# Retention recurrence in 64-token steps, with k in diagonal blocks and crossbar transposes from the fifth chunk on

**The chip, the cores and the metric.** One core of one Trainium2 chip. The metric is device microseconds of one execution; for each kernel the median of its runs is given, with the runs of the kernel before on the same chip beside it. Spans and times inside a trace are some 1.7 us shorter than the run's time.

## The reference

```python
# batch 8, heads 8, sequence 576, head_dim 64; d_model 512, d_ff 1536; float32
scores = q @ k.T / sqrt(64)
D[i, j] = gamma[h] ** (i - j) if i >= j else 0       # gamma[h] = 1 - 2 ** (-5 - h)
ret = (scores * D) @ v                               # per head
x = ret.transpose(0, 2, 1, 3).reshape(4608, 512)
out = (1 / (1 + exp(-(x @ w_gate))) * (x @ w_val)) @ w_out
```

Both kernels run the attention as a recurrence over chunks of 128 tokens, five to a batch (the last is a half chunk of 64). `gamma ** i` is multiplied into q and `gamma ** -j` into k, so that what is left of D is a triangle. Per chunk: scores (k against q), output (state times q, plus v times masked scores), and the state (sum of k times v). Chunks 0 to 3 are done in another way, which the change leaves alone. The rest of TensorE's time is the feed-forward part, in blocks of 128 to 512 tokens, between whose matmuls the chunk phases are placed. All matmuls are bf16.

## The kernel before

Heads are handled in pairs (two heads of 64 fill 128 rows or columns). Chunks 4 to 9 work in half-array tiles, on q and k that TensorE transposed. From chunk 10 on (`EARLY`), q and k are cast to bf16 on GpSimd, transposed by the DMA crossbar, and VectorE lays k^T out in diagonal blocks of two heads (`kbd`), so that a matmul uses the whole array.

```python
def cross(s):                                    # crossbar, from chunk 10 on
    for nm, bufs in (("k", 4), ("q", 5)):
        t = att_pool.tile([P, M, P], BF16, ...)
        nc.sync.dma_start_transpose(out=t[:, :, 0:n], in_=natural[nm, s][0:n]...)

def phase_kb(s):                                 # VectorE: k^T into diagonal blocks
    for hh in range(2):
        nc.vector.tensor_copy(out=kb[p0:p0 + 64, 0:nj, :, p0:p0 + 64]..., in_=kT[p0:p0 + 64, 0:M, 0:n]...)

# phase_qk, a full chunk:
    nc.tensor.matmul(qkp[:, mm, 0:128],   lhsT=kb[:, 0, m, :], rhs=qT[:, m, 0:128], ...)
    nc.tensor.matmul(qkp[:, mm, 128:192], lhsT=kb[:, 1, m, :], rhs=qT[:, m, 64:128], ...)
# phase_pv, for each pair m:
    (state[s - 1][:, m, :], qT[:, m, 0:128]), (vb[:, 0, m, :], pt[:, m, 0:128]), (vb[:, 1, m, :], pt[:, m, 128:192])
# phase_st: one step for 128 tokens
    nc.tensor.matmul(stp[:, m, :], lhsT=ks[:, 2*m:2*m+2, :], rhs=vn[:, 2*m:2*m+2, :], ...)

order += [("t", s + 1), ("pv", s), ("qk", s + 1), ("st", s + 1)]     # from chunk 10 on, s running
LEAD_LOAD = 5       # loads run five chunks ahead, casts two
# ... (cuts)
```

All loads, stores and crossbar transposes are issued by SyncE into one queue, in program order (half of the very last store aside).

## Time and profile before

| | before |
|---|---|
| time, median (lowest to highest) | 349.19 us (347.98 to 350.13), 4 runs |
| span of the profiled run | 346.6 us |
| TensorE busy | 338.1 us |
| GpSimd busy | 160.0 us |
| VectorE busy | 180.1 us |
| DMA packets; share of the 16 engines that the one queue takes | 147,506; 75.9% |

To read it: TensorE sets the time nearly everywhere, so what counts is each stretch in which it waits. The lines are in the prediction. Times in microseconds from the span's start place every event below.

### The profile page before, as it was taken

Reading aid. Unit: us, or ns where it says so; the run is one execution under the profiler, and the core shown is the slowest. Engines: PE = TensorE matmul, PEld = TensorE weight load, DVE = VectorE, ACT = ScalarE, POOL = GpSimd, SP = SyncE. Lnnn points to the kernel's source line nnn. Section 1 sums busy time; section 2 is a strip of 40 time slices with the busy share of each in tenths; the row PEclk is TensorE's granted clock in tenths of the full one; section 3 lists DMA queues with packets and bytes.
Section 4 is the critical chain, followed back from the end, with each engine's and each line's share of the span. In section 5 each row is a group of like instructions: output and inputs, shape, how many; then the busy total and the mean of one; then the engine's idle time right before and its main releaser. Section 6 shows DMA issues by size and latency. Waiting matters only on the chain.

```text
span 346.6 us, 7262 instructions
## 1 busy us (share of the span) xinstructions
PE 338.1 (98%) x2744; PEld 195.3 (56%) x2744; DVE 180.1 (52%) x365; ACT 129.2 (37%) x250; POOL 160.0 (46%) x264
## 2 busy tenths in 40 slices
PE   8899999899999999999999999999999999999996
PEld 3565447676856556656656655554555555544443
DVE  4655555595757646616736836552764355503320
ACT  6765414344334234233234334332333243324321
POOL 7743764778538736543366855533666400000000
PEclk9999999999999999999999999999999999999999
DMA  7999999999999999929829999929794410020002
GB/s 222 315 365 269 282 262 203 243 232 163 161 199 192 176 201 209 132 95 198 150 97 191 179 194 191 179 21 212 164 173 32 121 47 0 2 91 30 2 30 91
DMA packets 147506, 54.73 MB, mean 158 GB/s; under 512 B 130960, under 2 KB 139408, under 8 KB 147472
## 3 DMA queue, kind: packets, MB, share of 16 engines
q1 hardware_dynamic: 147328, 54.15, 75.9%
q8 instruction: 21, 0.34, 0.5%
q10 hardware_dynamic: 144, 0.13, 0.1%
q14 instruction: 13, 0.11, 0.1%
HBM read 37.75 MB, written 9.44 MB: 136 GB/s over the span
## 4 chain that ended last, share of the span: by engine, by line
PE 76%; DVE 2%; ACT 0%; issue 0%; ACTq 0%
PE h L567 44%; PE op L630 22%; PE pv L471 4%; PE qk L429 2%; PE st L492 2%; DVE kbd L397 1%; PE qk L431 1%; PE op L620 1%; DVE pte L418 0%; DVE qs L249 0%; DVE sbd L338 0%; DVE gv L585 0%; PE qk L438 0%; ACT g L580 0%; DVE sb L504 0%
## 5 line engine op out<-in xcount | busy, mean ns | idle before, releaser
L567 PE MATMUL h<-xT,wg_sb 128*128 128x512 bf16 (+3 forms) x592 | 118.0, 322 | 0.1
L567 PE MATMUL h<-xT,wv_sb 128*128 128x512 bf16 (+3 forms) x592 | 118.0, 322 | 0.1
L594 DVE TENSOR_TENSOR gv<-g,h 128x512 bf16<-128x512 bf16 (+1 forms) x104 | 65.0, 625 | 69.9 <-PE h L567 67.8
L590 ACT ACTIVATE g<-h 128x512 bf16<-128x512 f32 (+1 forms) x104 | 57.0, 548 | 100.1 <-PE h L567 80.3
L630 PE MATMUL op<-wo_sb,gv 128*128 128x512 bf16 x372 | 85.6, 379 | 0.0
L567 PEld LDWEIGHTS <-wg_sb 128*128 128x128 bf16 x592 | 52.9, 98 | 38.5 <-issue 0.7
L567 PEld LDWEIGHTS <-wv_sb 128*128 128x128 bf16 x592 | 52.3, 98 | 33.0 <-DVE wv_sb L209 0.7
L239 POOL TENSOR_TENSOR ks<-k,ktab 128x512 bf16<-128x512 f32 (+1 forms) x36 | 37.4, 1040 | 59.6 <-issue 18.6
L267 POOL CAST vbd<-v 64x256 bf16<-64x256 f32 x108 | 42.9, 397 | 41.5 <-PE pv L471 36.3
L630 PEld LDWEIGHTS <-gv 128*128 128x128 bf16 x372 | 34.9, 98 | 37.6
L602 ACT COPY ob<-op 128x512 f32<-128x512 f32 x35 | 20.3, 586 | 60.5 <-PE op L630 50.5
L433 DVE TENSOR_TENSOR pt<-qk,tri 128x384 bf16<-128x384 f32 x48 | 24.5, 551 | 35.3 <-PE qk L431 35.3
L249 POOL TENSOR_TENSOR qs<-q,qtab 128x512 bf16<-128x512 f32 (+1 forms) x30 | 32.3, 1075 | 1.1 <-DMA qT<-qs 1.0
L397 DVE COPY kbd<-kT 64x512 bf16<-64x512 bf16 (+1 forms) x60 | 28.2, 470 | 0.9
L472 ACT CAST xT<-pv 128x512 bf16<-128x512 f32 (+1 forms) x36 | 19.4, 538 | 21.9 <-PE pv L471 18.8
L258 POOL CAST vn<-v 128x512 bf16<-128x512 f32 (+1 forms) x36 | 23.9, 665 | 0.0
L504 DVE TENSOR_TENSOR sb<-st,bdm 128x512 bf16<-128x512 f32 x24 | 16.5, 687 | 5.8 <-PE st L492 5.8
L580 ACT ACTIVATE g<-h 128x256 bf16<-128x256 f32 x32 | 12.3, 384 | 17.3 <-PE h L567 13.4
L471 PE MATMUL pv<-pt,vbd 128*128 128x128 bf16 (+1 forms) x216 | 17.3, 204 | 0.0
L471 PEld LDWEIGHTS <-vbd 128*128 128x128 bf16 x216 | 14.7, 98 | 3.4
L471 PE MATMUL pv<-qT,sb 128*128 128x128 bf16 (+1 forms) x96 | 13.8, 213 | 0.0
L582 DVE TENSOR_TENSOR gv<-g,h 128x256 bf16<-128x256 bf16 x20 | 8.4, 418 | 10.2 <-ACT g L580 9.9
(92 smaller groups left out, 238.7 us busy)
## 6 DMA issues: line engine op xcount, KB each, us to landing
out_dram<-ob SPq DMA_DIRECT2D x35, 256.0 KB, 2.2
v<-in_v_dram SPq DMA_DIRECT2D x28, 256.0 KB, 4.1
k<-in_k_dram SPq DMA_DIRECT2D x28, 256.0 KB, 4.5
q<-in_q_dram SPq DMA_DIRECT2D x28, 256.0 KB, 5.1
wg<-in_moe_w_gate_dram SPq DMA_DIRECT2D x12, 256.0 KB, 5.5
wv<-in_moe_w_val_dram SPq DMA_DIRECT2D x12, 256.0 KB, 5.5
wo<-in_moe_w_out_dram SPq DMA_DIRECT2D x12, 256.0 KB, 5.6
k32p<-in_k_dram SPq DMA_DIRECT2D x4, 256.0 KB, 4.7
```

The source lines that it names most:

```text
L239: nc.gpsimd.tensor_tensor(out=ks[0:n], in0=k32[0:n], in1=ktab[0:n, c, :].unsqueeze(2).to_broadcast([n, H, D]), op=ALU.mult)
L249: eng.tensor_tensor(out=qs[0:n], in0=q32[0:n], in1=qtab[0:n, c, :].unsqueeze(2).to_broadcast([n, H, D]), op=ALU.mult)
L258: nc.gpsimd.tensor_copy(out=vn[0:n], in_=v32[0:n])
L267: nc.gpsimd.tensor_copy(out=vb[hh * 64:hh * 64 + 64, j, :, hh * 64:hh * 64 + 64], in_=v32[j * 64:j * 64 + 64, hh::2, :])
L397: nc.vector.tensor_copy(out=kb[p0:p0 + 64, 0:nj, :, p0:p0 + 64].rearrange("p j m t -> p m j t"), in_=kT[p0:p0 + 64, 0:M, 0:n].rearrange("p ...
L433: nc.vector.tensor_tensor(out=pt[:, 2 * g:2 * g + 2, :], in0=qkp[:, :, 0:192], in1=tri.unsqueeze(1).to_broadcast([P, 2, 192]), op=ALU.mult)
L471: nc.tensor.matmul(pvp[:, m, a:e], lhsT=w, rhs=x, start=(i == 0), stop=(i == len(mm) - 1))
L567: nc.tensor.matmul(out, lhsT=w_sb[:, kc, fc * P:(fc + 1) * P], rhs=xT[:, kc, t0 + a:t0 + e], start=(kc == 0), stop=(kc == NKC - 1))
L590: nc.scalar.activation(out=g[:, 0:n], in_=h1[:, 0:n], func=AF.Sigmoid)
L594: nc.vector.tensor_tensor(out=gvs[some[0]][:, a:e], in0=g[:, 0:n], in1=h2[:, 0:n], op=ALU.mult)
L602: nc.scalar.copy(out=ob, in_=opp)
L630: nc.tensor.matmul(opp, lhsT=gvs[fc][:, nb * P:(nb + 1) * P], rhs=wo_sb[:, fc, :], start=(fc == 0), stop=(fc == NFC - 1))
```

## The change

Its intent: spend fewer TensorE columns on the recurrence. With steps of 64 tokens every recurrence matmul is a full-array one of 64 columns; k is cast straight into diagonal blocks, which serve both the state step and, through the crossbar, the scores, so VectorE's copies go; and chunks 4 to 9 leave the half-array form.

```diff
 def cast_k(s):
-    nc.gpsimd.tensor_tensor(out=ks[0:n], in0=k32[0:n], in1=ktab..., op=ALU.mult)
+    for j in range(n // 64):
+        for hh in range(2):
+            nc.gpsimd.tensor_tensor(out=kn[half(hh), j, :, half(hh)], in0=k32[half(j), hh::2, :], in1=ktab..., op=ALU.mult)
 def cast_v(s):          # v also twice: in diagonal blocks (vbd) and plain (vs), 8 copies of 64x256
+                if c < NC - 1:
+                    nc.gpsimd.tensor_copy(out=vs[half(hh), j], in_=v32[half(j), hh::2, :])
 def cross(s):           # k: 128x1024 through the crossbar (512 before)
+    nc.sync.dma_start_transpose(out=t[:, 0:nj]..., in_=natural["k", s][:, 0:nj]...)
-def phase_tk, phase_tq, phase_kb
 def phase_qk(s):
+    for j in range(nj):
+        for m in range(M):
+            nc.tensor.matmul(qkp[:, m, half(j)], lhsT=kT[:, j, m, :], rhs=qT[:, m, half(j)], ...)
+def phase_st(s, j):     # two steps a chunk; VectorE copies the state after each
-order.append(("qk", s + 1)); order.append(("st", s + 1))
+order.append(("qk", s + 1)); order += [("st0", s + 1), ("st1", s + 1)]
 ...
+        if kind == "qk":
+            loads_to(s + LEAD_LOAD)     # LEAD_LOAD = 5, LEAD_CAST = 2
+            casts_to(s + LEAD_CAST)     # k, q, crossbar, v
 ...
+    loads_to(7)
+    casts_to(6)
+    loads_to(8)
```

(The triangle masks, the order of the wo loads and the first placements of phases also change.)

## The prediction

> **What bounds the kernel now.** I read the page first: busy shares, slices, chain.
>
> ```profile
> PE 338.1 (98%) x2744; PEld 195.3 (56%) x2744; DVE 180.1 (52%) x365; ACT 129.2 (37%) x250; POOL 160.0 (46%) x264
> ...
> PEclk9999999999999999999999999999999999999999
> DMA  7999999999999999929829999929794410020002
> ...
> PE 76%; DVE 2%; ACT 0%; issue 0%; ACTq 0%
> ```
>
> TensorE is busy 98% of 346.6 us at full clock and carries 76% of the chain: a column less on TensorE is time off the end. But the DMA row stands at 9 up to the sixteenth slice, some 139 us. The windows by stage (columns: us, then each engine's busy time, clock, DMA share, GB/s) say where that hurts.
>
> ```profile
> 36.00:60.00 24.00, 24.00 (x222) 12.98 (x220) 13.30 (x28) 7.99 (x16) 15.65 (x23) 1.00 1.07 251
> 60.00:92.00 32.00, 29.53 (x403) 23.30 (x397) 21.98 (x57) 12.28 (x29) 23.52 (x37) 1.00 1.05 206
> 92.00:140.00 48.00, 47.86 (x380) 29.58 (x378) 29.43 (x56) 17.19 (x35) 27.27 (x44) 1.00 1.13 192
> 140.00:260.00 120.00, 120.00 (x878) 67.84 (x876) 65.20 (x122) 41.69 (x77) 64.93 (x106) 1.00 0.84 155
> 260.00:346.00 86.00, 83.34 (x501) 41.74 (x498) 30.38 (x53) 26.54 (x46) 9.26 (x16) 1.00 0.17 45
> ```
>
> From 36 to 140 us TensorE and the DMA engines are both full. After that DMA has room. The only stage with real TensorE idleness is 60 to 92 us, 2.5 us of it.
>
> The price of a matmul is read from starts, not from the mean ns of a row, which includes the pipeline. The timeline of TensorE:
>
> ```profile
> 112.88 0.28 PE L438 MATMUL qk<-qT,kbd 128*128 128x64 bf16 x4
> 112.99 0.81 PE L567 MATMUL h<-xT,wv_sb 128*128 128x384 bf16 x4
> ```
>
> Four 64-column matmuls, each with new weights, take 112.99-112.88 = 0.11 us: 28.5 ns each. By the same reading a 128-column one takes 56 ns (the first three matmuls of a pv head pair, 128+128+64 columns, repeat every 0.14 us).
>
> **What the Trainium skill says.** "TensorE: Matmul & The Clock Gate", section "Wait — 56ns, not 53.3ns?": start to start is N/2.4 + about 2.5 ns, never under about 25 ns. That gives 55.8 and 29.2 ns; the trace agrees. The same page, "Back-to-back issue gap", says a stream of weight-load and matmul pairs sustains about 81 ns at N=128; the trace does not agree (56 ns), so I use 28.5 even for runs of small matmuls. "DMA: Bandwidth & Descriptors", "Queues, rings and completion order": each DMA engine consumes one issuer's descriptors in ring order. So a transpose waits behind loads issued before it; the trace agrees, with 4.1 us from issue to landing for kT. "TensorEngine Tiling (Array Packing)", "Key Properties": changing the tiling mode drains TensorE; the change removes such switches from chunk 4 on, and I count no more for them than the measured starts contain.
>
> **The change, part by part.** TensorE, per full chunk with an incoming state, chunks 10 on: before, scores 4x128+4x64, state 4x128, output 8x128+4x64 columns: 16x56+8x28.5 = 1.12 us. After: 8 score, 8 state, 16 output matmuls, all 64 wide: 32x28.5 = 0.91. Saved 0.21; a first chunk of a batch saves 0.10 (0.90 to 28x28.5 = 0.80), a half chunk nothing. Six batches x (3x0.212+0.102) = 4.4 us. The six chunks 4 to 9 now cost 8.4 us by starts (both transposes 2.7, scores 1.8, state 1.0, output 2.9). After: three chunks at 32, one at 28, two at 12 matmuls, 148x28.5 = 4.2. Saved 4.2. The TensorE gaps there (1.48 and 0.39 us before scores that wait for qT, 0.25 before a transpose, 1.0 at 85.7 before scores that wait for kbd, 0.3 at 111.8) are 3.4 us and their causes go. TensorE's gross gain: 12.0 us, 3.4%.
>
> VectorE loses the 60 kbd copies (28.2 us) and pays two 64x256 state copies per 64 tokens (4x0.42 = 1.7 us a chunk, against 0.69): even or lighter, and 48% idle. GpSimd: k becomes four pieces, about half of the 1.04 us each (estimate from the equal rows at 64 and 128 partitions), v eight copies at 0.44 (four took 1.75), q 1.04: 2.1+3.5+1.04 = 6.6 us a full chunk, before 4.4. Some 3 us a half chunk. All 36 chunks: 28x6.6+8x3 = 209, with weights and constants about 235 us. TensorE spends about 39 us on a batch of five chunks, GpSimd 29.5: it holds in the steady part.
>
> DMA: kT doubles, from 512 to 1024 packets of 256 bytes, and chunks 4 to 9, which now use no crossbar, get it. Before a full pair is 1024 packets, after 1536. A 256 KB load of 1024 packets takes 1.2 us in the full stretches (3,200 to 3,460 packets in 4 us), so the new pair costs 1.8 us, and 0.4 for the thin stretch that the packets show around transposes: 2.2 us, a half pair 1.1. A 2 KB-packet tile (wo, a store) takes 0.7. Steady cycle: 3x1.2+2.2+0.7 = 6.5 us under TensorE's 8.5: hidden. In the full stretch it is not hidden. The timelines of GpSimd, SyncE and TensorE there, in that order:
>
> ```profile
> 35.60 1.03 POOL L239 TENSOR_TENSOR ks<-k,ktab 64x512 bf16<-64x512 f32 x1 [5.24 <-DMA k<-in_k_dram]
> ```
>
> ```profile
> 77.21 1.67 SPq L276 DMA_TRANSPOSE kT<-ks  x1
> 78.99 2.85 SPq L276 DMA_TRANSPOSE qT<-qs  x1
> ```
>
> ```profile
> 58.01 0.40 PE L412 MATMUL qk<-qT,kT 64*128 64x128 bf16 x8
> ...
> 68.36 0.40 PE L412 MATMUL qk<-qT,kT 64*128 64x128 bf16 x8 [1.32 <-ACT qT L387]
> ...
> 73.51 0.40 PE L412 MATMUL qk<-qT,kT 64*128 64x128 bf16 x8 [0.23 <-ACT qT L387]
> ```
>
> k of chunk 4 lands at 35.6; the first crossbar transpose is issued at 77.2. My prices for what lies between (rest of load 4 0.6, load 5 3.6, twelve wo 8.3, loads 6 to 13 27, six stores 4.1) sum to 43.6, so 79.2, when its packets indeed begin (79.8). Now the new order from 35.6: q4 and load 5 to 39.8; five wo 43.3; T4 (the transposes of chunk 4) 44.4; five wo 47.8; T5 50.0; two wo, loads 6, 7 58.6; T6 60.8; loads 8, 9, 10 and three stores 71.9; T7 74.1; load 11, a store, T8 80.6; load 12, T9, a store 86.0; load 13, T10 91.8; a store, load 14, T11 96.5. One us more to land. The scores of chunks 6, 7, 8 then start at 61.8, 75.1, 81.6, where they were at 58.0, 68.4, 73.5. Scores 9 follow TensorE's own work, 6.8 us later, 88.4; scores 10 wait to 92.8 (86.8 before) and scores 11 start at 97.5 (92.1 before). So at chunk 11 the new kernel is 5.4 us behind, with its early savings already spent inside the waits. From there it gains the 4.4 of the later batches and the 0.3 gap. Net +0.7: 349.6 to 350.3, call it 350.
>
> **The rivals.** First, DMA is hidden after all: loads run up to five chunks ahead, so later loads may give way and the transposes land in time. Against it: loads 8 to 11 stand in the same queue before T7 and T8. For it: the new order of wo loads shows care for this stretch. Then the 12.0 us come in: 338. Second, the supply is worse: transposes cost the 0.8 us of thinned packets that several pairs show in the trace now, and the output matmuls of the first 512 tokens wait for wo, whose casts now follow eight v copies in GpSimd's order (v5 ends about 45.6, wo 2 wanted at 43.8). Each pair 0.5 more is 3 to 4 us by chunk 11, and idle TensorE may lose its clock: 355 to 359. Third, the two state steps of a chunk: the second may not overwrite the bank until VectorE has copied the first. In a 384-token block the phases lie 1.7 us apart and the copies need 0.84, so little; if it fails, up to 0.3 us x 28 chunks = 8 us, 358. Fourth, 64-column matmuls in runs of 16 fall to weight-load pace, say 50 ns: 964x21 = 20 us. The four in a row at 28.5 speak against it.
>
> **Range and chances.** The gain is solid arithmetic, the loss an estimate of queue times with a few us either way: 350, range 341 to 359. Faster by over 2% (below 342.6) needs nearly all of the supply loss to vanish: 0.17. Slower by over 2% (above 356.6) needs the second or third rival: 0.25. Within 2%: 0.58.
>
> **What would show it.** Right: TensorE's summed time for chunks 4 on falls from 36 to 27.5 us at 28.5 ns a matmul; TensorE waits at the scores of chunks 6, 7, 8 for the transposes, several us each; between 36 and 100 us its busy share drops to about 80 to 85%, after 110 us it stays over 99%; GpSimd about 235 us busy. Wrong: no waits at those scores (first rival), waits of state matmuls on VectorE in the steady blocks (third), starts over 35 ns (fourth), or a clock below full.

## The result, and the profile after

The changed kernel takes 358.22 us (357.85 to 359.3, 4 runs) against 349.19 us: slower, ratio 1.0266, 95% interval 1.0224 to 1.0307. A ratio here is the mean time of one kernel's runs over that of the other's of the same rounds, so it is not quite the ratio of the medians.

The page of the changed kernel (span 356.7 us): busy times, the clock and DMA in 40 slices, the chain by engine.

```profile
PE 333.6 (94%) x2833; PEld 192.2 (54%) x2868; DVE 162.1 (45%) x343; ACT 126.8 (36%) x245; POOL 225.9 (63%) x447
...
PEclk9999989969989999999999999999999999999999
DMA  7999999999999999983985999999699550011002
...
PE 72%; POOL 14%; DMA 7%; issue 3%; DVE 2%; ACT 1%; SPq 1%; POOLq 0%; ACTq 0%; DVEq 0%
```

TensorE has less to do and the span is 10 us longer, so TensorE waits. GpSimd and DMA are now on the chain, and the clock falls in the sixth, ninth and twelfth slices. The windows (the first number pair is the stretch, then its length, then each engine's busy time) say when:

```profile
60.00:100.00 40.00, 29.18 (x377) 24.37 (x380) 16.31 (x48) 9.75 (x24) 37.09 (x75) 0.88 1.09 202
100.00:140.00 40.00, 39.75 (x367) 25.10 (x369) 19.91 (x43) 14.82 (x31) 31.65 (x63) 0.99 1.10 189
140.00:260.00 120.00, 118.89 (x984) 67.18 (x995) 60.74 (x119) 42.17 (x80) 91.02 (x182) 1.00 0.94 175
```

From 60 to 100 us TensorE is busy 29.2 of 40 us (GpSimd 37.1), after that nearly always. TensorE's timeline shows the same stretch as waits ahead of scores (the bracket: idle just before, and what ended it):

```profile
61.61 0.39 PE L365 MATMUL qk<-qT,kT 128*128 128x64 bf16 x8 [2.17 <-DMA qT<-qs]
...
74.84 0.58 PE L365 MATMUL qk<-qT,kT 128*128 128x64 bf16 x8 [3.71 <-DMA qT<-qs]
...
82.74 0.39 PE L365 MATMUL qk<-qT,kT 128*128 128x64 bf16 x8 [1.47 <-DMA qT<-qs]
```

These are chunks 6, 7 and 8, waiting for a crossbar transpose. Starts of the scores, from the timelines:

| scores of chunk | 6 | 7 | 8 | 9 | 10 | 11 | end of span |
|---|---|---|---|---|---|---|---|
| before | 58.0 | 68.4 | 73.5 | 81.5 | 86.8 | 92.1 | 346.6 |
| predicted after | 61.8 | 75.1 | 81.6 | 88.4 | 92.8 | 97.5 | |
| after | 61.6 | 74.8 | 82.7 | 90.8 | 96.5 | 104.2 | 356.7 |
| after, loads four ahead (last experiment) | 62.7 | 72.0 | 78.2 | 85.8 | 91.3 | 99.2 | 351.4 |

So at chunk 11 the changed kernel is 12.1 us late; by the end 10.1. The question is what makes the transposes late. Two suppliers stand before them. GpSimd casts (two of its costliest groups on the page):

```profile
L227 POOL TENSOR_TENSOR kbd<-k,ktab 64x256 bf16<-64x256 f32 x128 | 78.3, 612 | 47.4 <-PE st L398 32.7
...
L252 POOL CAST vs<-v 64x256 bf16<-64x256 f32 x112 | 44.7, 399 | 0.0
```

and the queue of SyncE, whose timeline from chunk 6's transposes to chunk 7's is

```profile
56.87 1.24 SPq L261 DMA_TRANSPOSE kT<-kbd  x1
58.20 2.12 SPq L265 DMA_TRANSPOSE qT<-qs  x1
60.41 0.53 SPq L82 DMA_DIRECT2D v<-in_v_dram  x1
...
66.84 1.48 SPq L82 DMA_DIRECT2D q<-in_q_dram  x1
68.43 3.74 SPq L261 DMA_TRANSPOSE kT<-kbd  x1
```

Between 60.41 and 68.32 stand nine load instructions, the v, k and q of chunks 8, 9 and 10. Chunk 7's q had been cast by 64.9, as GpSimd's timeline shows (the first line is chunk 7's q, the second chunk 8's):

```profile
63.82 1.04 POOL L237 TENSOR_TENSOR qs<-q,qtab 128x512 bf16<-128x512 f32 x1
70.71 1.04 POOL L237 TENSOR_TENSOR qs<-q,qtab 128x512 bf16<-128x512 f32 x1
```

Put side by side for each chunk (GpSimd's q cast ends, SyncE's k transpose is issued; k itself is cast 1.1 us before q):

| chunk | 7 | 8 | 9 | 10 | 11 |
|---|---|---|---|---|---|
| cast done | 64.9 | 71.7 | 77.3 | 81.9 | 88.8 |
| transpose issued | 68.4 | 77.8 | 84.9 | 91.7 | 97.8 |

### The profile page after: what moved, and what is told of

Same layout as the page of the kernel before. It is cut to its first block, busy times and chain, and to the rows that moved or that the text cites. A ratio compares the mean times of both kernels' runs of the same rounds, so it can differ in the third digit from the quotient of the medians.

```text
span 356.7 us, 7632 instructions
## 1 busy us (share of the span) xinstructions
PE 333.6 (94%) x2833; PEld 192.2 (54%) x2868; DVE 162.1 (45%) x343; ACT 126.8 (36%) x245; POOL 225.9 (63%) x447
## 2 busy tenths in 40 slices
DMA packets 169396, 60.27 MB, mean 169 GB/s; under 512 B 152848, under 2 KB 161296, under 8 KB 169360
## 4 chain that ended last, share of the span: by engine, by line
PE 72%; POOL 14%; DMA 7%; issue 3%; DVE 2%; ACT 1%; SPq 1%; POOLq 0%; ACTq 0%; DVEq 0%
PE h L457 41%; PE op L520 21%; POOL kbd L227 6%; POOL vbd L250 3%; POOL vs L252 2%; POOL qs L237 2%; DMA qT<-qs 2%; DMA q<-in_q_dram 2%; PE qk L365 2%; PE st L398 2%; PE pv L386 2%; PE pv L384 2%; DMA k<-in_k_dram 1%; DMA q32p<-in_q_dram 1%; DVE sbd L404 1%
## 5 line engine op out<-in xcount | busy, mean ns | idle before, releaser
L227 POOL TENSOR_TENSOR kbd<-k,ktab 64x256 bf16<-64x256 f32 x128 | 78.3, 612 | 47.4 <-PE st L398 32.7
L520 PE MATMUL op<-wo_sb,gv 128*128 128x512 bf16 x356 | 84.1, 379 | 0.8
L367 DVE TENSOR_TENSOR pt<-qk,tri 128x512 bf16<-128x512 f32 (+1 forms) x36 | 22.7, 630 | 72.0 <-PE qk L365 71.7
L404 DVE CAST sbd<-st 64x256 bf16<-64x256 f32 x112 | 47.0, 420 | 14.9 <-PE st L398 12.5
L250 POOL CAST vbd<-v 64x256 bf16<-64x256 f32 x128 | 50.7, 396 | 4.4
L252 POOL CAST vs<-v 64x256 bf16<-64x256 f32 x112 | 44.7, 399 | 0.0
L365 PE MATMUL qk<-qT,kT 128*128 128x64 bf16 x256 | 13.6, 195 | 10.4 <-DMA qT<-qs 10.4
L365 PEld LDWEIGHTS <-kT 128*128 128x128 bf16 x256 | 12.7, 99 | 17.1 <-DMA kT<-kbd 9.2
L398 PEld LDWEIGHTS <-kbd 128*128 128x128 bf16 x224 | 13.5, 100 | 13.2 <-DVE sbd L404 5.1
L386 PE MATMUL pv<-pt,vbd 128*128 128x64 bf16 x256 | 19.5, 194 | 0.0
L384 PE MATMUL pv<-qT,sbd 128*128 128x64 bf16 x228 | 18.5, 195 | 0.1
```

Source lines behind the costliest of these rows:

```text
L227: nc.gpsimd.tensor_tensor(out=kn[half(hh), j, :, half(hh)], in0=k32[half(j), hh::2, :], in1=ktab[half(j), c, hh::2].unsqueeze(2).to_broadc ...
L250: nc.gpsimd.tensor_copy(out=vb[half(hh), j, :, half(hh)], in_=v32[half(j), hh::2, :])
L252: nc.gpsimd.tensor_copy(out=vs[half(hh), j], in_=v32[half(j), hh::2, :])
L365: nc.tensor.matmul(qkp[:, m, half(j)], lhsT=kT[:, j, m, :], rhs=qT[:, m, half(j)], start=True, stop=True)
L384: nc.tensor.matmul(pvp[:, m, half(j)], lhsT=before[:, m, :], rhs=qT[:, m, half(j)], start=True, stop=False)
L386: nc.tensor.matmul(pvp[:, m, half(j)], lhsT=vb[:, j, m, :], rhs=pt[:, m, half(j)], start=before is None, stop=True)
```

## The experiments

The theory at first: the early chunks (36 to 105 us) are short of supply, GpSimd and the DMA queue together, and the rest of the change works as meant. Rivals: the lost clock is a cost of its own; the two state steps of a chunk wait for VectorE; the 64-column matmuls are slow.

### One: GpSimd without the second copies of v

Wrong result: `vs` is a constant, which takes four of eight v copies per chunk off GpSimd.

```diff
-        vs = nat_pool.tile([P, 2, M, D], BF16, tag="vs", ...)
+        vs = vs0                                  # memset once
-                if c < NC - 1:
-                    nc.gpsimd.tensor_copy(out=vs[half(hh), j], ...)
```

> The changed kernel without the four extra copies of v for the state (their tile is a constant, so the result is wrong on purpose); GpSimd then needs 5.3 us a full chunk instead of 6.9. If GpSimd's casts set when the transposes start, each of the waits at the scores of chunks 6, 7, 8 and 10 shrinks by 1.5 us or more and the whole comes to 350 us or less. If the queue of transfers sets it (transposes behind loads and other transposes), only the 2 us wait of the first output matmuls for wo goes, and the time stays at 354 to 357 us.

Measured: 357.81 us, ratio 1.0255 (1.0223 to 1.0287), which is 0.4 us less than the changed kernel and within the spread of both, although GpSimd fell from 225.9 to 188.6 us. (It lies 0.8 us above the range foreseen for the queue.) TensorE's wait for wo shrinks from 1.84 to 0.38 us, so that the scores of chunk 4 start at 46.5 us instead of 49.0, but by chunk 6 nothing is left of it (61.5 against 61.6). Chunk 7's transpose was issued at the same time as before:

```profile
68.30 4.03 SPq L261 DMA_TRANSPOSE kT<-kbd  x1
```

What follows: GpSimd by itself is not the bound.

### Two: half of k through the crossbar

Wrong result: the first 64 tokens' transposed k serves both halves.

```diff
-        nc.sync.dma_start_transpose(out=t[:, 0:nj]..., in_=natural["k", s][:, 0:nj]...)
+        nc.sync.dma_start_transpose(out=t[:, 0:1]..., in_=natural["k", s][:, 0:1]...)
-    lhsT=kT[:, j, m, :]
+    lhsT=kT[:, 0, m, :]
```

> The changed kernel with only the first 64-token half of each k tile sent through the crossbar, and used for both halves (wrong on purpose): the transposes are as small as in the kernel before, GpSimd's work is unchanged. If the queue of transfers sets the starts: five pairs before the scores of chunk 8 each 0.5 to 0.6 us shorter, chunk 10 some 4 us earlier, one or two losses of clock fewer: 350 to 354 us. If GpSimd sets them: 357 to 359 us, as it was.

Measured: 354.7 us, ratio 1.0171 (1.0137 to 1.0206), 3.5 us less than the changed kernel. Scores of chunk 11 start at 100.0 instead of 104.2. Packets fall from 169,396 to 155,060. Neither forecast range holds 354.7. So the doubled k costs about 3.5 us when it alone is taken away, and that is less than half of the loss.

### Three: transposes ahead of the loads

Correct; an order change only.

```diff
         if kind == "qk":
-            loads_to(s + LEAD_LOAD)
             casts_to(s + LEAD_CAST)
+            loads_to(s + LEAD_LOAD)
...
-    loads_to(7)
     casts_to(6)
+    loads_to(7)
     loads_to(8)
```

> The changed kernel with the crossbar transposes of a chunk issued ahead of the loads that read further ahead (T6 before loads 7 and 8, T7 before load 10, and so on). If what delays them is their place in the queue behind loads: T7 is issued near 65 us, when GpSimd has q7, instead of 68.4, and T8 near 72 instead of 77.8; the waits at the scores of chunks 7 and 8 lose 3 to 5 us together and the time is 351 to 355 us. If the transfers are bound by their sheer amount in this stretch, the loads that are put back delay later chunks as much: 357 us or more.

Measured: 356.85 us, ratio 1.0223 (1.0188 to 1.0258), 1.4 us gained, with intervals that overlap; neither forecast range holds it. I first took this to mean that order is worth nothing. The trace shows a fault of the experiment instead: load 7 now stood behind the transposes of chunk 6, which wait for a cast, and SyncE issued nothing from 51.7 to 57.3 us.

```profile
49.72 1.96 SPq L82 DMA_DIRECT2D q<-in_q_dram  x1
57.29 1.23 SPq L261 DMA_TRANSPOSE kT<-kbd  x1
```

So chunk 7 was as late as before (68.3), for another reason.

### Four: keeping the clock

Correct; dummy matmuls fill the waits (7 before the third group of the first output block, 8, 15, 6 and 10 before the scores of chunks 6, 7, 8 and 10).

```diff
+    WAITS = {6: 8, 7: 15, 8: 6, 10: 10}
+            if s in WAITS:
+                keep(WAITS[s])                    # zeros, 128x512
             phase_qk(s)
```

> The changed kernel with dummy matmuls put into its long waits (7 before the third wo group, 8, 15, 6 and 10 before the scores of chunks 6, 7, 8 and 10; each 0.216 us, less than the wait it fills). If the three stretches at half clock are a second cost of the waits: the granted clock is 1.0 throughout, and 4 to 5 us are gained: 353 to 355 us. If the work slowed in those stretches would have waited for the transfers anyway: 357 to 359 us.

Measured: 358.9 us, ratio 1.029 (1.0249 to 1.0331). The mean clock rose from 0.981 to 0.995 in the profiled runs and the time did not fall. The scores of chunks 6, 7, 8, 10 and 11 start at 61.5, 74.7, 84.1, 97.9 and 104.0. TensorE's timeline at chunks 8 and 10 (`keep` are the dummies):

```profile
84.12 0.59 PE L374 MATMUL qk<-qT,kT 128*128 128x64 bf16 x8 [2.70 <-DMA qT<-qs]
...
95.75 2.32 PE L143 MATMUL keep<-blank 128*128 128x512 bf16 x10
97.91 0.40 PE L374 MATMUL qk<-qT,kT 128*128 128x64 bf16 x8
```

Keeping most of the clock bought nothing. That the lost clock costs nothing is not shown by this run alone: chunk 8's transpose landed 1.4 us later than in the changed kernel, the dummies held the scores of chunk 10 some 1.0 us beyond the landing of theirs, and from scores 10 to scores 11 TensorE took 6.1 us where it took 7.7 with a half-clock stretch inside. That the cost is small is what the changed kernel's own four runs suggest: their mean clocks go from 0.981 to 0.990, and their times do not follow (358.44 us at 0.981, 358.0 and 359.3 at 0.990).

### Five, seven and eleven: the late part alone

The kernel before up to chunk 9, the changed form from chunk 10 on. Correct, all three. Five keeps the changed order (both state steps follow the scores, and the phase that VectorE's k copies had is left empty):

```diff
-    order: t(s+1), pv(s), qk(s+1), st(s+1)                # 128-token steps
+    order: t(s+1), pv(s), qk(s+1), st0(s+1), st1(s+1)     # from chunk 10 on, 64-token steps; t is empty
```

> One part alone: chunks 4 to 9 as in the kernel before (half-array tiles, transposes on TensorE), steps of 64 tokens with k in diagonal blocks from chunk 10 on. If the loss is the supply of the early chunks: the kernel before less 4.4 us of matmuls plus up to 2 us of state steps waiting for VectorE: 344 to 347 us, and no score wait over 1 us. If the 64-token steps are themselves the loss (small matmuls, two state steps a chunk): 351 us or more.

Measured: 351.82 us, ratio 1.0088 (1.0048 to 1.0129): a miss. Its list of waits (total us, times, longest) names the reason:

```profile
PE st L503 <- DVE sbd L509: 3.8, 6, 0.7
...
PEld L503 <- DVE sbd L509: 10.7, 16, 1.2
```

The second state step of a chunk waits for VectorE's copy of the first, 0.3 to 0.7 us a time on the matmuls and up to 1.2 on their weight loads. Seven puts the chunk's output between the two:

```diff
-    qk(s+1), st0(s+1), st1(s+1)
+    pv(s), st1(s), qk(s+1), st0(s+1)                      # no empty phases
```

> The version with early chunks as before and steps of 64 tokens from chunk 10 on, with the second state step of a chunk moved behind the chunk's output, and the empty phases taken out, so that a phase of matmuls and feed-forward work lies between any two state steps. In the version without this TensorE waited 6.5 us for VectorE's state copies, in ten waits up to 0.9. If those waits are what the 64-token steps give back, they go and the time is 344 to 347 us, faster than the kernel before by about 1%. If the steps lose for another reason, it stays at 351 to 352.

Measured: 345.24 us (344.16 to 348.61, 6 runs), ratio 0.9913 (0.9873 to 0.9953): faster than both kernels, though by less than the 2% at which the verdict would say so, and 6.6 us below the run that differs only in order and in the empty phases (their shares of the 6.6 are not separated). Its profiled run was the slowest of the six (348.61 us), so its trace shows what is left and not the gain. What is left in its early part is a wait of the old form, scores of chunk 7 (the kernel before has it with 1.32 us):

```profile
69.81 0.40 PE L444 MATMUL qk<-qT,kT 64*128 64x128 bf16 x8 [2.93 <-ACT qT L416]
```

ScalarE's copy of q stood behind a copy of a finished output block, which waited for a free store buffer. Eleven adds one:

```diff
-    osb_pool = ctx.enter_context(tc.tile_pool(name="osb", bufs=4))
+    osb_pool = ctx.enter_context(tc.tile_pool(name="osb", bufs=5))      # vn and vs three deep, for the room
```

> The mixed kernel (chunks 4 to 9 as before, 64-token steps from chunk 10 on, second state step behind the output) with a fifth buffer for output stores, so that ScalarE's copy of a finished output block does not hold the qT copy of chunk 7 behind it (3.1 us of TensorE idle at 66.7 us in the trace of the mixed kernel). If that wait is lost time: 342 to 344 us. If TensorE then waits for the next thing in the full stretch, 345 us as without it.

Measured: 344.1 us (343.69 to 348.26, 6 runs), ratio 0.9885 (0.9843 to 0.9927). The wait fell to

```profile
67.48 0.40 PE L444 MATMUL qk<-qT,kT 64*128 64x128 bf16 x8 [0.23 <-ACT qT L416]
```

This is the best version found. Its interval overlaps that of seven, so that the fifth buffer made it faster is likely from the trace and not settled by the times. What follows from the three: where the two state steps are apart, the 64-token steps gain 3.3 us (345.24 against 348.5 in the same rounds) of the 4.4 that their matmul time was put at.

### Six: the early part alone

Crossbar from the fifth chunk on and no half-array tiles, but steps of 128 with VectorE's k copies, as the kernel before has them from chunk 10 on. Correct.

```diff
-    PAIRED .. EARLY: half-array chunks
+    order = [t(4), qk(4)], then t(s+1), pv(s), qk(s+1), st(s+1) from chunk 4 on
```

> The other part alone: all chunks from the fifth on through the crossbar and no half-array tiles, but steps of 128 tokens as in the kernel before (k through the crossbar undoubled, VectorE makes the diagonal blocks, GpSimd 4.4 us a chunk). If the supply is the loss and doubling k makes it worse: chunks 6 to 8 still wait, but less; TensorE saves 3.5 us of early matmuls; 348 to 352 us. If the 64-token steps are the loss: 346 us or less, with no waits at the early scores.

Measured: 359.34 us, ratio 1.0301 (1.0266 to 1.0336). A miss: it is no faster than the changed kernel, and neither forecast range holds it. I had not tuned where its phases stand, and VectorE copies that waited for the crossbar (4.0, 7.4 and 6.1 us) held back others behind them, as TensorE's waits show:

```profile
PE qk L378 <- DVE kbd L362: 7.3, 3, 4.8
PE op L554 <- DVE gv L509: 5.8, 1, 5.8
```

So chunks 4 to 9 wait for the crossbar even with k transposed once; how much of the 11 us is the crossbar's and how much my placement's is not separated.

### Eight: both orders in the changed kernel

Three, with the state steps apart as in seven. Correct.

```diff
+    pv(s), st1(s), qk(s+1), st0(s+1)              # on top of run three
```

> The changed kernel with transposes ahead of loads and the second state step behind the chunk's output. On top of the run with the transposes first alone, the waits of state matmuls for VectorE go (some 3 us of them in the changed kernel): 2 to 3 us less than that run if those waits were on the path, the same if they hid behind the transposes.

Measured: 357.0 us, ratio 1.0231 (1.0199 to 1.0263), the same as three. In the changed kernel the state waits are not the thing to mend first; run three's fault is in this one too.

### Nine and ten: both supplies relieved

Runs one and two together, and then with the orders of eight on top. Wrong results.

```diff
+    vs = vs0                                      # as run one
+    t[:, 0:1], kT[:, 0, m, :]                     # as run two
```

> The changed kernel with both supplies relieved at once: no vs copies on GpSimd (as in the first experiment) and only one half of k through the crossbar (as in the second); the result is wrong on purpose. Singly these gave about 0.4 and 3.5 us. If GpSimd and the DMA queue bind in alternation, so that each hides the relief of the other, together they give clearly more than the sum: 347 to 352 us, with scores of chunk 7 before 72 us and of chunk 11 before 98 us. If the two are independent costs, 354 us. If something else holds the early chunks (TensorE's own order), 354 us or more and chunk 11 still at about 100 us.

> As the run before, and the casts and transposes of a chunk are ordered ahead of the later loads, and the second state step of a chunk follows its output (the order that helped elsewhere); wrong on purpose. If the early supply is the whole loss and the 64-token steps are worth their matmul time, this is the changed kernel with its loss taken away: about 343 to 347 us, below the kernel before. If order is worth nothing once supply is relieved, as the run before. At 353 or more the supply theory falls.

Measured: 355.65 us, ratio 1.0202 (1.0159 to 1.0244), and 355.94 us, ratio 1.0196 (1.0156 to 1.0236). Neither comes near the 343 to 352 us of the theory that two supplies hide each other, and it falls: nine is no better than two, with the scores of chunk 11 at 101.6 us. Nine's chunks 7 to 11 issue their k transposes at 67.1, 76.0, 82.6, 89.5 and 95.1 us, those of run two at 67.9, 76.5, 83.1, 89.5 and 95.2, though in run nine q of chunk 7 was cast by 62.6. So with GpSimd early, the queue keeps the time. And ten shows what the misplaced load 7 did; its window (DMA share is the number before the last):

```profile
52.00:60.00 8.00, 5.69 (x69) 3.89 (x68) 1.87 (x7) 3.41 (x7) 5.03 (x9) 1.00 0.44 78
```

The DMA engines, at over 1.0 in the windows on both sides, stood at 0.44 here, some 5 us of transfers (8 us times 0.66) lost in the stretch that lacks them. The theory left: the transposes are late because loads of chunks wanted later stand before them in the one queue.

### Twelve: fewer loads ahead

Correct; the changed kernel with loads four chunks ahead, behind the casts of their phase, and load 7 left ahead of the transposes of chunk 6.

```diff
-    LEAD_LOAD = 5
+    LEAD_LOAD = 4
         if kind == "qk":
-            loads_to(s + LEAD_LOAD)
             casts_to(s + LEAD_CAST)
+            loads_to(s + LEAD_LOAD)
...
     loads_to(7)
     casts_to(6)
-    loads_to(8)
```

> The changed kernel, correct, with one thing moved: loads run four chunks ahead instead of five and are issued behind the casts and transposes of the same phase, while load 7 stays ahead of the transposes of chunk 6 (in the run that put transposes first it had moved behind them). In the changed kernel GpSimd had q of chunks 7 to 11 ready at 64.9, 71.7, 77.3, 81.9 and 88.8 us, but their transposes were issued at 68.4, 77.8, 84.9, 91.7 and 97.8: 3.5 to 10 us later, behind the loads of chunks 10 to 14 in the same queue. If the loads ahead in the queue are what holds the transposes, these are issued 3 to 8 us earlier, the scores of chunk 11 start near 95 to 98 us (104.2), and the time is 347 to 352 us. If GpSimd holds them, nothing moves: 357. If the k buffers (three, each held until the state step of its chunk) hold them, GpSimd waits for state matmuls and about half is gained: 353 to 355.

Measured: 350.74 us (349.9 to 353.1, 7 runs) against 348.98 us, ratio 1.0043 (1.0013 to 1.0073). Of the changed kernel's 9.0 us over the kernel before (358.22 - 349.19) 1.8 are left. Same packets (169,396), the same instructions in another order; GpSimd has 226.1 us of work as before. The lead, the order within a phase and the place of load 8 changed together; what each is worth was not measured. SyncE's timeline:

```profile
64.95 1.24 SPq L261 DMA_TRANSPOSE kT<-kbd  x1
...
72.49 1.78 SPq L261 DMA_TRANSPOSE kT<-kbd  x1
...
93.23 2.62 SPq L261 DMA_TRANSPOSE kT<-kbd  x1
```

Chunks 7, 8 and 11 are issued 3.5, 5.3 and 4.6 us earlier, and the scores of chunk 11 start at 99.2, 5.0 us earlier. The profiled run was the slowest of the seven (353.1 us), so this trace shows less of the gain than the median does. Most of it is won by chunk 7: between its transposes and chunk 6's stand three load instructions (61.30 to 63.80 us) instead of nine. After that, chunk 7's transposes to chunk 11's take 28.3 us, 29.4 before. What holds it now is mixed. GpSimd is one part: chunk 7's k transpose is issued as soon as its k cast, the first line below, has ended. Later GpSimd has to wait for a k buffer, which a state step frees (second line):

```profile
62.29 2.64 POOL L227 TENSOR_TENSOR kbd<-k,ktab 64x256 bf16<-64x256 f32 x4
...
81.48 2.64 POOL L227 TENSOR_TENSOR kbd<-k,ktab 64x256 bf16<-64x256 f32 x4 [2.25 <-PE st L398]
```

and one state step waits 2.34 us for VectorE at 76.2. A version with this order and the state steps apart was not run; whether it would beat 344 us is open.

## Why the prediction was right or wrong

The time was put at 350 and was 358.2, inside the range of 341 to 359 but near its end; "within 2%" was given 0.58 and "slower" 0.25. The mechanism was right, the balance of its two terms was not. Point by point:

- **TensorE's saving: right in kind.** 64-column matmuls run in long rows without a fall to half pace: the sixteen output matmuls of chunk 8 start between 85.97 and 86.44 us, 29 ns each. Eleven, which has none of the early saving, gains 3.7 us from the scores of chunk 11 (92.8 against 92.1) to the end (343.6 against 346.6), where the prediction had 4.4 and 0.3 for the later part. The fourth rival falls.
- **The early saving is spent inside waits: right.** The scores of chunks 6, 7 and 8 were predicted at 61.8, 75.1 and 81.6 and started at 61.6, 74.8 and 82.7, after waits for transposes of 2.2, 3.7 and 1.5 us. From 36 to 100 us TensorE was busy 78% of the time (80 to 85% foreseen). From 140 to 260 us TensorE was busy 99.1%, as foreseen.
- **"So at chunk 11 the new kernel is 5.4 us behind": this term failed. It was 12.1.** Up to chunk 8 the queue's prices held within 1.1 us; then each step was too cheap. The queue was given 80.6 to 96.5, or 15.9 us, from chunk 8's transposes to chunk 11's; their issues were 20.0 apart (77.8 to 97.8). That is 1.4 us a chunk more than my 5.3, in place of the 0.5 that the second rival allowed. By the time that each held SyncE, the price that was too small is that of a pair of transposes. SyncE's timeline shows the pair of chunk 9, a half chunk, which was put at 1.1 us:

```profile
84.87 3.19 SPq L261 DMA_TRANSPOSE kT<-kbd  x1
88.16 1.19 SPq L265 DMA_TRANSPOSE qT<-qs  x1
89.40 0.57 SPq L82 DMA_DIRECT2D v<-in_v_dram  x1
```

It held SyncE 4.5 us (84.87 to 89.40), and those of chunks 10 and 11 held it 3.4 and 3.1, put at 2.2 each: 11.0 us in place of 5.5. The loads and stores between them took 8.6 in place of 10.4. How much of such a hold is the transpose's own, and how much is owed to the loads issued before it, is not separated. Then "scores 11" was given 4.7 us after scores 10 as if only the transfer counted. It took 7.7 (96.5 to 104.2) with no wait before it: TensorE's own work, 5.3 in the kernel before (86.8 to 92.1) and 6.1 where the clock was kept (97.9 to 104.0), with a stretch of 3.4 us at half clock in it.
- **"From there it gains the 4.4 of the later batches and the 0.3 gap": half. It gained 2.0** (12.1 to 10.1). The third rival may be part of it: in the changed kernel the weight loads of state steps wait 5.1 us in all for VectorE's copies, their matmuls 1.4. But run eight, with the steps apart, was no faster than run three, so where the missing 2.7 us went is not shown.
- **The first rival named the lever and I gave it too little weight.** "Later loads may give way": they do not by themselves, since the queue is in order, but moving them is possible and takes off 7.5 us (358.2 to 350.7, run twelve). The doubled k transposes, on which I put the loss, are worth 3.5 us singly.
- **GpSimd:** 225.9 us against 235 predicted. A k piece took 612 ns against about 520, a v copy 397 against 440, and the casts sum to 211 us against 209; the weights and constants took less than allowed. In the changed kernel it was not the bound (run one).
- **Clock:** below full for 13.6 us in three stretches, as the second rival feared. Keeping most of it gained nothing (run four); one of the stretches lies in the 7.7 us above.
- **Slips in the working that change nothing:** 0.11 us for four matmuls is 27.5 ns and not 28.5 (in the trace's unrounded times the starts lie 29 ns apart); the DMA row stands at 9 up to the seventeenth slice; and TensorE idles as much from 260 to 346 us (2.7 us, at the very end) as from 60 to 92. The drain at a change of tiling mode, which the prediction cites, was measured by no run.

## What to carry to other kernels

Where one in-order queue carries both loads for later and transfers wanted now, compare for each transfer the time its data was ready with the time it was issued; a gap of several us points to the queue, and here a faster producer did not mend it (runs one and nine). Once the order is mended, look at the producer again (run twelve). How far loads run ahead is a price paid by everything behind them, so run them only as far ahead as the consumer needs. And when a reordering gains nothing, look in the trace for what the new order made wait before concluding that order is worth nothing.

## What the Trainium skill lacked or had wrong

- "TensorE: Matmul & The Clock Gate", section "Back-to-back issue gap", gives about 81 ns per weight-load and matmul pair at 128 columns. In the kernel before such pairs repeat at 56 ns, and pairs of 64 columns at about 29.
- The same page, section "HAM oscillation — how this bites in real kernels", states the rule as no idle gaps over about 3.4 us. In the changed kernel a half-clock stretch began at 46.3 us, in the second of two waits of 0.41 and 1.84 us, and another at 97.5 us after one of 2.54: shorter waits were enough. (The section after it tells of short idles with that effect, without their length.) Nor does it say that keeping the clock may gain nothing: here the time was 358.9 us with most of it kept and 358.2 with 13.6 us at half clock.
- "DMA: Bandwidth & Descriptors", section "DMA Transpose (X-bar)", has no time that a transpose between SBUF tiles holds its issuer. Here it held SyncE 1.2 us at the least, and up to 3.7 us for the 1024-column one in the full stretch; nor does the section say that loads issued ahead delay it (9.0 us from cast to issue for chunk 11).
